# Recutting the last weight load and moving three output products ahead of it in a DMA-bound decode kernel

## The chip, the cores and the metric

The kernel runs on one core of a Trainium2 chip. The metric is the device time of one execution in microseconds (us), the median of several; lower is better. Executions of one kernel scatter by up to about half a microsecond, so differences under that are read from the traces rather than from the times.

The engines are named as in the profile: PE does matmuls, PEld is its weight loads, DVE and ACT are the vector and scalar engines, SP issues the loads. A "row" below means one row of a weight matrix per partition, 128 x 576 numbers in bf16. It takes two matmuls, one for each half of the 576 columns.

## The reference, cut to what matters

```python
x = A_x                                              # (1, 1, 576)
g = _sigmoid((x * gate_w).sum(-1, keepdims=True))
a = _A_ref(x, A_k_cache, A_v_cache, A_wq, A_wo)      # windowed attention, last step: o @ wo
b = _B_ref(x, B_w1, B_b1, B_w2, B_b2)                # gelu(x @ w1 + b1) @ w2 + b2
return g * a + (1 - g) * b                           # (1, 1, 576)
```

One token is decoded. Nearly everything is weights and cache that are read once: 53.6 MB. The last two matrices read are `wo` (4096 x 576) and the second half of `w2` (2304 x 576, so 18 rows on each of 128 partitions).

## The kernel before

The output is a bias and a sum of 68 rows into one accumulator, `y_ps`; each row is a vector column times a weight row. The two halves go to different column tiles of PE.

```python
    def y_add(vec, row, start=False, stop=False):
        for s in range(2):
            last = nc.tensor.matmul(
                y_out[s], lhsT=vec, rhs=row[:, s * DH : (s + 1) * DH],
                start=start, stop=stop, skip_group_check=True,
            )
        return last
```

The end of the stream of loads, all from one queue and in this order:

```python
    for r0, r1 in ((0, 16), (16, RO)):                       # RO = 32
        nc.sync.dma_start(out=wo_t[:, r0:r1, :], in_=wo_src[:, r0:r1, :])
    for j0, j1 in ((0, 10), (10, 16), (16, 18)):             # NJ = 18
        nc.sync.dma_start(out=w2_t[:, NJ + j0 : NJ + j1, :], in_=w2_src[:, 1, j0:j1, :])
```

And the order in which PE takes the rows. Eight rows of `wo` (8 to 15) land with the first half of it but are held back, so that PE has something to do while it waits:

```python
    late = [(gt, f, w2_t[:, f, :]) for f in range(6, NJ)]
    wo_at = [(ov, r, wo_t[:, r, :]) for r in range(RO)]
    w2_at = [(gt, f, w2_t[:, f, :]) for f in range(NJ, NF)]
    late += wo_at[0:8] + wo_at[16:RO] + wo_at[8:13] + w2_at[0:10] + wo_at[13:16] + w2_at[10:]
    before = ov_mm
    for n, (vec, at, row) in enumerate(late):
        with tc.issue_after(before.ins):
            before = y_add(vec[:, at : at + 1], row, stop=(n == len(late) - 1))
    ...
    nc.scalar.copy(out=out_row[:, DH:D], in_=y_out[1])
    nc.vector.tensor_copy(out=out_row[:, 0:DH], in_=y_out[0])
    nc.sync.dma_start(out=out.rearrange("a b d -> (a b) d"), in_=out_row[:])
```

Of the kernel before, what the change touches and what calls it, by code (L numbers as in the profile page):

```python
# [18 lines left out]
def kernel(  # L19
# [564 lines left out]
    RO = Hq * Dh // P  # L584
    wo_t = big.tile([P, RO, D], BF16, name="wo_t", tag="D")
    wo_src = A_wo.rearrange("(p r) n -> p r n", r=RO)
    for r0, r1 in ((0, 16), (16, RO)):
        nc.sync.dma_start(out=wo_t[:, r0:r1, :], in_=wo_src[:, r0:r1, :])  # L588
    for j0, j1 in ((0, 10), (10, 16), (16, 18)):
        nc.sync.dma_start(out=w2_t[:, NJ + j0 : NJ + j1, :], in_=w2_src[:, 1, j0:j1, :])  # L590

    om = const.tile([P, Hq, 4], BF16, name="om")
# [13 lines left out]
    late = [(gt, f, w2_t[:, f, :]) for f in range(6, NJ)]  # L606
    wo_at = [(ov, r, wo_t[:, r, :]) for r in range(RO)]
    w2_at = [(gt, f, w2_t[:, f, :]) for f in range(NJ, NF)]
    late += wo_at[0:8] + wo_at[16:RO] + wo_at[8:13] + w2_at[0:10] + wo_at[13:16] + w2_at[10:]
    before = ov_mm  # L610
    for n, (vec, at, row) in enumerate(late):
        with tc.issue_after(before.ins):
# [36 lines left out]
```

## Time and profile before

| what | before |
|---|---|
| time, median (range) | 132.39 us (132.32 to 132.78), 3 runs |
| span of the profiled run | 130.7 us |
| share of 16 DMA engines used by the load queue | 96.4% |
| PE busy | 79.9 us, 61% |
| chain's last load ends | 127.84 us |
| matmuls behind it | 16, 1.19 us |

How to read it: a queue that holds 96% of the DMA engines means that the kernel is as long as its transfers plus what cannot run beside them. At the end, that is whatever PE must still do with the rows that land last. So the views that matter are the chain of waits, read from its end, and the timeline of PE over the last ten microseconds. The prediction below shows the lines of both.

Beside the views I use the trace's list of landings: each load adds one to a semaphore for each of 16 DMA engines, and the trace holds the time of each increment.

### The profile page before, as it was taken

To read this page: it belongs to the slowest core of one execution; us is meant where nothing else is said; L and a number is where in the kernel's file an instruction comes from. 1 tells how busy PE (TensorE), PEld (TensorE's weight loads), DVE (VectorE), ACT (ScalarE), POOL (GpSimd) and SP (SyncE) were. 2 spreads that over 40 slices of the span, in tenths; PEclk is the share of its full clock that TensorE was granted. 3 is DMA by queue.
4 is the path that set the end of the run, shared out by engine and by line. 5 is a ranking of instruction groups with operands and counts; after the bars stand their busy time and mean duration, and the time that the engine had idled before them with its cause. 6 is when DMAs were issued, how large, how long until landed. Compare 5 with 4: busy or idle time off the path is not lost.

```text
span 130.7 us, 2382 instructions
## 1 busy us (share of the span) xinstructions
PE 79.9 (61%) x1138; PEld 46.0 (35%) x1071; DVE 51.9 (40%) x47; ACT 8.1 (6%) x17; POOL 8.2 (6%) x28
## 2 busy tenths in 40 slices
PE   0037999466002998859909986987100930999573
PEld 0037949366000121211201121677000920945441
DVE  0053000400069969999999995604000010010001
ACT  3000000002100000030003003020000000000001
POOL 6029600000000000000000000000000000000000
PEclk9999999999999999999995999965555555556999
DMA  7999999899899999999999999999989999999980
GB/s 220 431 442 423 474 422 474 372 451 466 381 426 471 401 411 471 411 411 471 421 411 451 441 401 441 413 417 458 456 381 441 461 386 407 434 422 422 398 330 24
DMA packets 2468, 53.75 MB, mean 411 GB/s; under 512 B 278, under 2 KB 282, under 8 KB 540
## 3 DMA queue, kind: packets, MB, share of 16 engines
q1 hardware_dynamic: 2450, 53.61, 96.4%
q8 instruction: 8, 0.13, 0.4%
q10 hardware_dynamic: 10, 0.01, 0.0%
HBM read 53.62 MB, written 0.00 MB: 410 GB/s over the span
## 4 chain that ended last, share of the span: by engine, by line
DMA 54%; DVE 24%; PE 13%; issue 6%; SPq 1%; DVEq 0%
DMA k_t<-in_A_k_cache_dram 27%; DMA w_t<-in_B_w_dram 26%; DVE kt L441 19%; PE s_ps L463 7%; PE o_ps L543 5%; DVE m L479 3%; DVE pt L512 2%; PE y_ps L306 1%; SPq L588 1%; DVE mr L482 1%; PE mt_ps L488 0%; DVE out_row L617 0%; SPq L172 0%; SPq L590 0%; SPq L168 0%
## 5 line engine op out<-in xcount | busy, mean ns | idle before, releaser
L463 PE MATMUL s_ps<-kt,qz_flat 128*128 128x512 bf16 x128 | 32.3, 409 | 17.3 <-DVE kt L441 10.4
L441 DVE STREAM_TRANSPOSE kt<-k_t 128x4096 f32<-128x4096 f32 x8 | 35.3, 4432 | 11.8 <-DMA k_t<-in_A_k_cache_dram 10.7
L543 PE MATMUL o_ps<-pt,v_t 128*128 128x8 bf16 x512 | 14.2, 167 | 16.7 <-DMA v_t<-in_A_v_cache_dram 15.4
L463 PEld LDWEIGHTS <-qz_flat 128*128 128x128 bf16 x64 | 6.8, 106 | 40.1 <-issue 40.0
L543 PEld LDWEIGHTS <-v_t 128*128 128x128 bf16 x512 | 14.1, 103 | 17.5 <-DMA v_t<-in_A_v_cache_dram 15.6
L334 PE MATMUL h_ps<-x,w_t 128*128 128x2 bf16 x162 | 10.4, 202 | 0.0
L334 PEld LDWEIGHTS <-w_t 128*128 128x128 bf16 x162 | 10.2, 162 | 0.5 <-issue 0.4
L306 PE MATMUL y_ps<-w_t,gt 128*1 128x288 bf16 x72 | 7.4, 361 | 1.1 <-DMA w_t<-in_B_w_dram 1.1
L500 ACT ACTIVATE p_t<-s_ps,negm 128x1024 bf16<-128x1024 f32 x4 | 4.5, 1114 | 50.6 <-DVE negm L496 50.6
L573 DVE RECIPROCAL rg<-mt_ps 128x32 f32<-128x32 f32 x1 | 0.4, 358 | 15.8 <-PE mt_ps L568 15.8
L512 DVE STREAM_TRANSPOSE pt<-p_t 128x1024 bf16<-128x1024 bf16 x4 | 4.9, 1224 | 2.7 <-ACT p_t L500 2.7
L372 PE MATMUL q_ps<-x,wq_t 128*128 128x2 bf16 x144 | 4.0, 166 | 3.1 <-DMA wq_t<-in_A_wq_dram 3.1
L306 PE MATMUL y_ps<-wo_t,ov 128*1 128x288 bf16 x64 | 4.9, 299 | 1.4 <-DMA wo_t<-in_A_wo_dram 1.4
L343 DVE COPY hacc<-h_ps 128x36 f32<-128x36 f32 x1 | 0.2, 196 | 13.2 <-PE h_ps L334 13.2
L617 DVE CAST out_row<-y_ps 1x288 bf16<-1x288 f32 x1 | 0.4, 445 | 12.3 <-PE y_ps L306 12.3
L479 DVE TENSOR_REDUCE m<-s_ps 128x1 f32<-128x1024 f32 x4 | 4.8, 1196 | 1.1 <-PE s_ps L463 1.1
L255 PE MATMUL xs_ps<-one_b,rows 1*128 1x1 bf16 x9 | 0.7, 196 | 7.2 <-DVE rows L249 7.2
L372 PEld LDWEIGHTS <-wq_t 128*128 128x128 bf16 x144 | 3.9, 104 | 3.2 <-DMA wq_t<-in_A_wq_dram 3.2
L306 PEld LDWEIGHTS <-gt 128*1 128x1 bf16 x72 | 3.6, 97 | 3.8 <-issue 1.9
L306 PEld LDWEIGHTS <-ov 128*1 128x1 bf16 x64 | 3.1, 90 | 2.9 <-issue 1.7
L593 DVE TENSOR_TENSOR om<-o_ps,rgh 128x128 bf16<-128x128 f32 x1 | 0.3, 291 | 8.6 <-PE o_ps L543 8.6
L249 DVE COPY rows<-rows 1x1152 bf16<-1x1152 bf16 x1 | 0.7, 748 | 6.4 <-DMA rows<-in_A_x_dram 6.4
(64 smaller groups left out, 33.5 us busy)
## 6 DMA issues: line engine op xcount, KB each, us to landing
k_t<-in_A_k_cache_dram SPq DMA_DIRECT2D x4, 4096.0 KB, 33.8
v_t<-in_A_v_cache_dram SPq DMA_DIRECT2D x4, 4096.0 KB, 23.3
wq_t<-in_A_wq_dram SPq DMA_DIRECT2D x1, 4608.0 KB, 26.1
wo_t<-in_A_wo_dram SPq DMA_DIRECT2D x2, 2304.0 KB, 30.0
w_t<-in_B_w_dram SPq DMA_DIRECT2D x1, 2880.0 KB
w_t<-in_B_w_dram SPq DMA_DIRECT2D x1, 2592.0 KB
w_t<-in_B_w_dram SPq DMA_DIRECT2D x1, 2304.0 KB, 8.0
w_t<-in_B_w_dram SPq DMA_DIRECT2D x1, 1440.0 KB
```

What stands on the lines that cost most here:

```text
L249: nc.vector.tensor_copy(out=xdup.rearrange("p (d t) -> p d t", t=2), in_=x_row.rearrange("p (d o) -> p d o", o=1).to_broadcast([1, D, 2]),)
L306: last = nc.tensor.matmul(y_out[s], lhsT=vec, rhs=row[:, s * DH : (s + 1) * DH], start=start, stop=stop, skip_group_check=True,)
L334: nc.tensor.matmul(h_ps[:, j:NF:NJ], lhsT=w1_t[:, i, j:FH:NJ], rhs=x2[:, i, :], start=False, stop=(i == NI - 1 and j == NJ - 1), skip_grou ...
L372: nc.tensor.matmul(q_ps[:, j : Hq : Hq // 2], lhsT=wq_t[:, i, j * Dh : (j + 1) * Dh], rhs=x2[:, i, :], start=(i == 0 and j == 0), stop=(i ...
L441: lambda: nc.vector.transpose(out=kt[g, f][:].bitcast(FP32), in_=keys.rearrange("p c d -> p (c d)").bitcast(FP32),),
L463: last = nc.tensor.matmul(s_ps[g][:, u * 512 : (u + 1) * 512].rearrange("p (c k) -> p c k", k=32), lhsT=qz(g, j, 2 * f + half), rhs=kv[:, ...
L479: queue("dve", lambda: nc.vector.reduce_max(out=m1[:], in_=s_ps[g][:], axis=AX.X))
L482: lambda: nc.vector.tensor_scalar(out=mr[:], in0=hi16[:], scalar1=m1[:, 0:1], scalar2=None, op0=ALU.mult),
L500: nc.scalar.activation(out=p_t[:].rearrange("p c k -> p (c k)"), in_=s_ps[g][:], func=ACT.Exp, bias=negm[:, 0:1], scale=SCALE, accum_out=s ...
L512: lambda: nc.vector.transpose(out=pt[:, g, :, :].rearrange("p c q -> p (c q)"), in_=p_t[:].rearrange("p c k -> p (c k)"),),
L543: last = nc.tensor.matmul(o_ps[:, 8 * g : 8 * g + 8, 0], lhsT=v_t[g][:, c, :], rhs=pt[:, g, c % 32, 8 * (c // 32) : 8 * (c // 32) + 8], st ...
L588: nc.sync.dma_start(out=wo_t[:, r0:r1, :], in_=wo_src[:, r0:r1, :])
```

## The change

The intent: the first of the three pieces gets 12 rows instead of 10, so that less is left for the pieces behind it, and all eight held rows run ahead of the first piece, so that PE is free when the pieces land.

```diff
-    for j0, j1 in ((0, 10), (10, 16), (16, 18)):
+    for j0, j1 in ((0, 12), (12, 16), (16, 18)):
         nc.sync.dma_start(out=w2_t[:, NJ + j0 : NJ + j1, :], in_=w2_src[:, 1, j0:j1, :])
@@
-    late += wo_at[0:8] + wo_at[16:RO] + wo_at[8:13] + w2_at[0:10] + wo_at[13:16] + w2_at[10:]
+    late += wo_at[0:8] + wo_at[16:RO] + wo_at[8:16] + w2_at
```

## The prediction

> **What bounds the kernel now.** I read the page first, from the share of each engine down to the chain that ended last, then the timeline of the end, where the change lies.
>
> ```profile
> span 130.7 us, 2382 instructions
> PE 79.9 (61%) x1138; PEld 46.0 (35%) x1071; DVE 51.9 (40%) x47; ACT 8.1 (6%) x17; POOL 8.2 (6%) x28
> ...
> DMA  7999999899899999999999999999989999999980
> GB/s 220 431 442 423 474 422 474 372 451 466 381 426 471 401 411 471 411 411 471 421 411 451 441 401 441 413 417 458 456 381 441 461 386 407 434 422 422 398 330 24
> ...
> q1 hardware_dynamic: 2450, 53.61, 96.4%
> ```
>
> The row of DMA digits is 8 or 9 nearly from end to end, and one queue holds 96.4% of all that the 16 DMA engines could do. The kernel is a stream of 53.6 MB. What is not hidden behind it is the start and what follows the last landing. No engine comes near: the busiest, PE, has 61%.
>
> The chain of waits says the same of the end. Its columns are start, duration, and what it was:
>
> ```profile
> 93.23 34.61 DMA w_t<-in_B_w_dram
> 127.84 0.04 issue
> 127.89 1.19 PE y_ps L306 x16
> 129.07 0.43 DVE out_row L617
> ```
>
> From 93.23 to 127.84 us the chain is only the load of the last matrix (the second half of w2, 18 rows per partition). After it come 16 matmuls, the copy of the result and the store. The timeline of PE shows the same stretch:
>
> ```profile
> 122.29 2.74 PE L306 MATMUL y_ps<-wo_t,ov 128*1 128x288 bf16 x42 [1.35 <-DMA wo_t<-in_A_wo_dram]
> 125.77 1.39 PE L306 MATMUL y_ps<-w_t,gt 128*1 128x288 bf16 x20 [0.74 <-DMA w_t<-in_B_w_dram]
> 126.99 0.54 PE L306 MATMUL y_ps<-wo_t,ov 128*1 128x288 bf16 x6
> 127.89 1.15 PE L306 MATMUL y_ps<-w_t,gt 128*1 128x288 bf16 x16 [0.36 <-DMA w_t<-in_B_w_dram]
> ```
>
> A row is two matmuls. So: 21 output rows (the second half of wo and five of the eight held back), a wait of 0.74 us, the 10 rows of the first w2 piece, the last three held rows, a wait of 0.36 us, and the last 8 rows, 6 of the second piece and 2 of the third.
>
> This view hides one thing. The last 16 matmuls look like one block behind the second piece, because no idle time lies between them. The trace's list of landings (one semaphore increment for each of 16 DMA engines) has the last increments at 125.727 us for the first piece, 127.844 for the second and 128.578 for the third. The first matmul that waits for each starts at 125.769, 127.885 and 128.619, each 0.041 to 0.042 us later. At the pace of 0.122 us a row (a row starts at 128.372, the next at 128.494) the third piece's first row would have started at 128.616 anyway. So the second and the third piece are both binding, to within 0.003 us. That decides this case.
>
> **What the Trainium skill says.** (1) "DMA: Bandwidth & Descriptors", section "Why a DMA increments its semaphore by 16 and not by 1": the engines finish separately, and only the sixteenth increment means that the data is there. The trace agrees: the first piece's increments run from 123.794 to 125.727 us, and PE moves 0.042 us after the last. (2) The same page, "Queues, rings and completion order": each DMA engine takes its descriptors in ring order. Then cutting the same rows elsewhere does not alter what each engine moves before its very last byte. The trace fits: the pieces land in the order of issue, all issued before 95 us. (3) "TensorE: Matmul & The Clock Gate", "Part 3: Packing small matmuls", "The mechanism": matmuls in different tiles of the array run beside each other, their starts about 4 ns apart. The two halves of a row go to different column tiles, and the trace shows them starting at 125.890 and 125.894 us. So a row, not a matmul, is the unit of cost. (4) The same page, "What's actually happening": the clock drops to half after an idle window of about 3.4 us and comes back after a busy one. Here the granted clock was 0.50 for 34.13 us, up to 120.07 us, and 1.00 after it. That matters for one rival.
>
> **The change part by part.**
>
> *Piece sizes.* 10, 6 and 2 rows become 12, 4 and 2. Bytes, number of loads, issue order and number of packets (128 a piece) stay. The packet records give medians of 435, 266 and 95 ns for 11,520, 6,912 and 2,304 bytes. From the first two, 169 ns for 4,608 bytes, or 85 ns for the two rows that move from one packet to another. The first piece's packet grows to about 520 ns, the second's falls to about 181; the sum is unchanged. The first piece lands later: its two extra rows take 2 x (127.844 - 125.727) / 6 = 0.706 us, so 126.433. By the packets it is 8 packets on each engine x 85 = 0.68 us, nearly the same. The second piece ends at the same row 16 as before: 127.844. The third: 128.578.
>
> *Order.* The comparison of the two programs' instructions has as many on each engine; on PE only the places of six output matmuls change, with their weight loads. The three held rows, formerly between the first and second pieces, now run ahead of the first. So, with R = 0.122 us a row:
>
> Before, starts of what follows the last row: first piece 125.769 + (10 + 3 + 8) R = 128.33; second 127.885 + 8 R = 128.86; third 128.619 + 2 R = 128.86. The latest decides: 128.86.
>
> After: the held rows are ready and have time: 24 rows from 122.29 end issuing at 122.29 + 24 R = 125.22, well ahead of 126.433. Then: first piece 126.433 + 0.042 + (12 + 4 + 2) R = 128.67; second 127.885 + 6 R = 128.62; third 128.619 + 2 R = 128.86. The latest decides: again 128.86.
>
> In order of time: PE waits for the first piece from about 125.40 (last result) to 126.475, does 12 rows until 127.94, finds the second piece there (127.885, so its wait goes), does 4 rows until 128.43, and is held for the third until 128.619. The wait of 0.36 us is not won. Idle before the first piece grows from 0.74 to about 1.07 us, and 0.19 us of pace is held up at the third piece (only some 0.03 us of it appears as idle, since a matmul's span of about 0.285 us covers the rest). The sum is 0.00 us. PE has gained 0.19 us of room in front of a landing that it cannot move.
>
> **The rivals.**
>
> *The gain is real (-0.05 to -0.19 us).* In the old kernel PE has no slack at the third piece: where the second lands late relative to the third, PE's 6 rows (0.73 us) end the program. The new kernel needs only 4 rows there. The interval between those landings is 0.734 us in this one execution; if in others it is shorter, the change wins the difference, up to 0.19 us or 0.14%. For it: the exact tie. Against it: the last packets come at the DMA engines' pace, 8 packets x 95 = 0.76 us on each, which has little reason to shrink. It would give about 132.3.
>
> *PE becomes the bound (+0.1 to +2 us).* The path behind the first landing now has only 0.19 us of room. If the first piece lands 0.2 us later than worked out, each further tenth counts. Much worse would be half clock: rows then cost 0.244 us, and the end would be 126.475 + 18 x 0.244 = 130.87, against 125.769 + 21 x 0.244 = 130.89 of the old order; both lose 2 us alike. Only if the longer single wait dropped the clock at the next step, 126.90 us (120.07 + 2 x 3.413), would the new kernel lose alone: about 3.5 rows done, 14.5 x 0.244 = 3.54 us to go, 130.44, so 1.6 us or 1.2%. Against it: the stretch 120.07 to 123.49 has PE busy for 2.07 of 3.42 us and was followed by full clock; the stretch up to 126.90 would still have about 2.34 of 3.41.
>
> ```profile
> 120.07:123.49 3.42, 2.07 (x33) 1.32 (x31) 0.00 (x0) 0.00 (x0) 0.00 (x0) 1.00 1.00 414
> 123.49:126.90 3.41, 2.67 (x46) 1.79 (x42) 0.00 (x0) 0.00 (x0) 0.00 (x0) 1.00 0.91 372
> ```
>
> (Columns: stretch, length, busy of PE, PEld, DVE, ACT and POOL, granted clock, DMA share, GB/s.)
>
> *The transfers themselves change (-0.2 to +0.2 us).* Other packet sizes might run differently beside each other at the end. The durations are nearly proportional to the bytes and the number of packets is equal, so I give it little.
>
> **Range and chances.** I predict the old median, less a trifle for the first rival: 132.37 us. The three times before lie between 132.32 and 132.78, so the scatter of single runs (0.46 us) is larger than any effect worked out here; a range of 132.1 to 132.75 covers the gain of 0.19, a loss of about that much, and the scatter. A change of 2% is 2.65 us. The DMA stream forbids that gain, as all waits in the stretch together are 0.74 + 0.36 = 1.10 us; the worst rival costs 1.6 to 2. So 0.985 for within 2%, 0.005 faster, 0.01 slower.
>
> **What would show it right or wrong.** In the new profile: one block of 48 output matmuls from about 122.3 us; idle of about 1.07 us before the first w2 block, which starts near 126.47; no wait of note for the second piece; the last four matmuls start at the third landing plus 0.04 us, which stays near 128.6; and the chain's last DMA now ends at the third landing, near 128.6 instead of 127.84, with about 0.45 us of matmuls behind it. Wrong if the last landing itself moves by more than 0.2 us, if the granted clock falls below 1.00 behind 122 us, or if the first piece lands behind 126.65, so that PE runs without a stop from it to the end.

## The result, and the profile after

The changed kernel took 132.44 us (132.37 to 132.56, 4 runs), the kernel before in the same rounds 132.41 us (132.32 to 132.78, 4 runs). The ratio is 0.9998, 95% interval 0.9977 to 1.0019: the same. (A ratio is the mean time of one kernel's fast runs over the mean of the other's fast runs of the same rounds, so it is not quite the ratio of the medians quoted.)

The page of the changed kernel, its span, granted PE clock, DMA and load queue:

```profile
span 130.6 us, 2382 instructions
...
PEclk9999999999999999986999999995555555557999
DMA  6999999899799899999989989899989989999980
...
q1 hardware_dynamic: 2450, 53.61, 96.3%
```

The trace has no record of the clock before 43.98 us, so the digits ahead of it are not a reading: matmuls of one form, 128x512, start 0.427 us apart just before that time and 0.217 us apart just after it, as if the clock had been half until then.

The stream is as full as it was: 96.3% of the DMA engines, the same number of packets and bytes. The end of the chain of waits (start, duration, what):

```profile
92.76 33.55 DMA w_t<-in_B_w_dram
126.31 0.04 issue
126.36 2.12 PE y_ps L306 x32
128.48 0.02 issue
128.50 0.45 PE y_ps L306 x4
```

And the timeline of PE (start, duration, operation, count, and in brackets the idle time before it and what ended it):

```profile
122.19 3.10 PE L306 MATMUL y_ps<-wo_t,ov 128*1 128x288 bf16 x48 [1.73 <-DMA wo_t<-in_A_wo_dram]
126.36 2.56 PE L306 MATMUL y_ps<-w_t,gt 128*1 128x288 bf16 x36 [1.06 <-DMA w_t<-in_B_w_dram]
```

Where there were two waits, 0.74 and 0.36 us, there is one of 1.06 us; where there were four blocks of matmuls, there are two. The order did what it was written for: all 24 output rows run as one block, and PE then works through all 18 rows of the last matrix without a visible stop. And the end is where it was.

The views hide why. The chain steps from the first piece's landing (126.31 us) straight to the end, as if PE's 36 matmuls were the bound. But there is a step of 0.02 us called "issue" at 128.48, just ahead of the last four matmuls. The list of landings explains it. In us from the start of the span:

| kernel | 1st piece landed | 2nd | 3rd | third piece's first row starts | after its landing | copy of the result starts |
|---|---|---|---|---|---|---|
| before | 125.727 | 127.844 | 128.578 | 128.619 | 0.041 | 129.063 |
| after | 126.312 | 127.726 | 128.458 | 128.501 | 0.043 | 128.943 |

In both kernels the last two rows start as soon as the last piece has landed, and not before. In the new one the row ahead of them starts at 128.189, so at the pace of 0.122 us PE was ready at 128.311 and was held up for 0.19 us. The view shows only 0.02 us of that as idle, because a matmul's span in it (about 0.285 us) reaches far beyond the time after which the next could start. The landings of the "after" trace are all about 0.1 us early, those of the second half of `wo` too (122.148 against 122.249), which no part of the change touches: scatter between executions.

The granted clock of the last stretches (columns: stretch, length, busy of PE, PEld, DVE, ACT, POOL, granted clock, DMA share, GB/s) stayed full through the longer wait:

```profile
122.49:125.90 3.41, 2.81 (x46) 1.89 (x43) 0.00 (x0) 0.00 (x0) 0.00 (x0) 1.00 0.98 405
125.90:129.31 3.41, 2.53 (x36) 1.52 (x35) 0.37 (x1) 0.33 (x1) 0.00 (x0) 1.00 0.35 138
```

### The profile page after: what moved, and what is told of

It reads as the page before. It is cut to its first block, busy times and chain, and to the rows that moved or that the text cites. A ratio compares the mean times of both kernels' runs of the same rounds, so it can differ in the third digit from the quotient of the medians.

```text
span 130.6 us, 2382 instructions
## 1 busy us (share of the span) xinstructions
PE 78.9 (60%) x1138; PEld 45.3 (35%) x1071; DVE 51.9 (40%) x47; ACT 8.1 (6%) x17; POOL 8.2 (6%) x28
## 3 DMA queue, kind: packets, MB, share of 16 engines
q1 hardware_dynamic: 2450, 53.61, 96.3%
## 4 chain that ended last, share of the span: by engine, by line
DMA 61%; DVE 21%; PE 10%; issue 6%; SPq 1%; DVEq 0%
DMA k_t<-in_A_k_cache_dram 31%; DMA w_t<-in_B_w_dram 26%; DVE kt L441 15%; PE o_ps L543 5%; DMA rows<-in_A_x_dram 4%; PE s_ps L463 3%; DVE m L479 3%; PE y_ps L306 2%; DVE pt L512 2%; SPq L588 1%; DVE mr L482 1%; DVE out_row L617 0%; PE mt_ps L488 0%; DVE negm L496 0%; DVEq L441 0%
## 5 line engine op out<-in xcount | busy, mean ns | idle before, releaser
L306 PE MATMUL y_ps<-wo_t,ov 128*1 128x288 bf16 x64 | 4.4, 286 | 1.7 <-DMA wo_t<-in_A_wo_dram 1.7
```

Source lines behind the costliest of these rows:

```text
L306: last = nc.tensor.matmul(y_out[s], lhsT=vec, rhs=row[:, s * DH : (s + 1) * DH], start=start, stop=stop, skip_group_check=True,)
```

## The experiments

The theory: the end is the last landing, plus 0.041 us, plus the rows that stand behind that landing (two, 0.122 us each), plus copy and store. PE's own work is hidden up to 0.19 us ahead of that. The rivals: PE's work from the first landing is the bound; or the sizes of the pieces change the transfers; or nothing on PE matters at all. The runs below were made on three occasions, each with its own runs of the kernel before (132.32, 132.57 and 132.38 us median). All results were correct against the reference. The smaller effects are read from the intervals and, above all, from the traces, each of which is one execution.

### One part of the change at a time

**The order alone**, with the old pieces:

```diff
-    for j0, j1 in ((0, 12), (12, 16), (16, 18)):
+    for j0, j1 in ((0, 10), (10, 16), (16, 18)):
```

> The new order with the old pieces of 10, 6 and 2 rows (R = 0.122 us a row). My theory, that the last landing (L3) plus 0.041 us plus two rows sets the end: the second piece is 6 rows and L2 + 0.041 + 8 R ties with L3 + 0.041 + 2 R, so 132.4 us, ratio 1.000. PE waits for about 0.33 us before the first piece (from about 125.4 to 125.7), runs its 10 rows, then waits for about 0.75 us for the second piece, and the last two rows start within 0.02 us of L3 + 0.041. Rival, that the order alone is worth something (the held rows filled a hole usefully): 0.1 to 0.4 us slower.

Measured: 132.40 us (5 runs), ratio 1.0004 (0.9991 to 1.0018). The timeline of PE in this run:

```profile
122.15 3.10 PE L306 MATMUL y_ps<-wo_t,ov 128*1 128x288 bf16 x48 [1.74 <-DMA wo_t<-in_A_wo_dram]
125.63 1.39 PE L306 MATMUL y_ps<-w_t,gt 128*1 128x288 bf16 x20 [0.37 <-DMA w_t<-in_B_w_dram]
127.74 1.14 PE L306 MATMUL y_ps<-w_t,gt 128*1 128x288 bf16 x16 [0.72 <-DMA w_t<-in_B_w_dram]
```

The two waits trade lengths, 0.74 and 0.36 for 0.37 and 0.72, and their sum stays. The last two rows start at 128.472, 0.042 us behind the third landing (128.430). The order by itself is worth nothing, and costs nothing.

**The sizes alone**, with three held rows still behind the first piece:

```diff
-    late += wo_at[0:8] + wo_at[16:RO] + wo_at[8:16] + w2_at
+    late += wo_at[0:8] + wo_at[16:RO] + wo_at[8:13] + w2_at[0:12] + wo_at[13:16] + w2_at[12:]
```

> The new pieces of 12, 4 and 2 rows with three held output rows still between the first and the second piece. My theory: first landing + 0.042 + (12 + 3 + 6) R = about 0.18 us behind L3 + 0.041 + 2 R, so PE runs without a stop from the first piece to the end, the first row of the third piece starts about 0.2 us (0.15 to 0.25) after its landing instead of 0.04, and the time is 0.18 us over the kernel before (ratio 1.001, under what five rounds resolve; the trace decides). Rival, that any order does since the stream is the bound: third piece's first row again at L3 + 0.04 us.

Measured: 132.55 us (5 runs), ratio 1.0020 (1.0007 to 1.0032), so 0.26 us over the kernel before. Its timeline of PE:

```profile
126.65 1.63 PE L306 MATMUL y_ps<-w_t,gt 128*1 128x288 bf16 x24 [1.44 <-DMA w_t<-in_B_w_dram]
128.12 0.54 PE L306 MATMUL y_ps<-wo_t,ov 128*1 128x288 bf16 x6
128.48 0.90 PE L306 MATMUL y_ps<-w_t,gt 128*1 128x288 bf16 x12
```

From the first landing on PE never waits again. The third piece landed at 128.735 us and its first row started at 128.973, 0.238 us later instead of 0.041: a loss of 0.20 us, where 0.18 was worked out. With these sizes and the old order PE is the bound. So the bigger first piece needs the new order, which then merely takes the loss away again.

### How much room PE has, and where

**Eight idle rows ahead of the first piece**: output products with a zero vector, which leave the sum as it is.

```diff
+    zv = const.tile([P, 1], BF16, name="zv")
+    nc.gpsimd.memset(zv[:], 0.0)
-    late += wo_at[0:8] + wo_at[16:RO] + wo_at[8:16] + w2_at
+    late += wo_at[0:8] + wo_at[16:RO] + wo_at[8:16]
+    late += [(zv, 0, wo_t[:, n, :]) for n in range(8)] + w2_at
```

> The new kernel with eight more rows of output products, against a zero vector, ahead of the first piece: 8 R = 0.98 us more PE work. My theory: it lies in the wait of 1.06 us before the first landing, so the time stays (ratio 1.000, 132.4 us), and the wait shrinks to about 0.1 us. Rival, that PE work near the end costs what it takes: 0.98 us more, ratio 1.0074.

Measured: 132.41 us (5 runs), ratio 1.0008 (0.9996 to 1.0021); 1.0074 is ruled out. The timeline of PE, in which 0.05 us of the wait is left where about 0.1 was expected:

```profile
125.22 1.15 PE L306 MATMUL y_ps<-wo_t,zv 128*1 128x288 bf16 x16
126.42 2.53 PE L306 MATMUL y_ps<-w_t,gt 128*1 128x288 bf16 x36
```

A whole microsecond of added work vanished in the wait ahead of the first piece, and the third piece's first row still started 0.042 us behind its landing (128.547 and 128.505).

**The same eight rows ahead of the last two:**

```diff
-    late += wo_at[0:8] + wo_at[16:RO] + wo_at[8:16] + w2_at
+    late += wo_at[0:8] + wo_at[16:RO] + wo_at[8:16] + w2_at[0:16]
+    late += [(zv, 0, w2_t[:, NJ + n, :]) for n in range(8)] + w2_at[16:]
```

> The new kernel with the same eight extra rows placed just ahead of the last two rows. My theory: PE has 0.19 us of room before the third landing, so 0.98 - 0.19 = 0.79 us more (ratio 1.006), and the third piece's first row starts 0.83 us after its landing. Rival, that PE is hidden behind the stream throughout: ratio 1.000. Rival, that PE has no room there, being the bound from the first landing: 0.98 us, ratio 1.0074.

Measured: 133.17 us (5 runs), ratio 1.0070 (1.0057 to 1.0084). The times do not tell 0.79 us (1.0060) from 0.98 us (1.0074); the trace does. Its timeline of PE:

```profile
126.39 2.12 PE L306 MATMUL y_ps<-w_t,gt 128*1 128x288 bf16 x32 [1.07 <-DMA w_t<-in_B_w_dram]
128.34 1.15 PE L306 MATMUL y_ps<-w_t,zv 128*1 128x288 bf16 x16
129.32 0.41 PE L306 MATMUL y_ps<-w_t,gt 128*1 128x288 bf16 x4
```

The third piece landed at 128.483 and its first row started at 129.323, 0.840 us later. Less the usual 0.042 that is 0.80 us of loss for 0.98 us of work: the room is 0.18 us, as worked out. The same work is free at one place and costs four fifths of its length at another, in a kernel in which the DMA engines are 96% busy.

### What stands behind the last landing

**Two pieces, 12 and 6 rows:**

```diff
-    for j0, j1 in ((0, 12), (12, 16), (16, 18)):
+    for j0, j1 in ((0, 12), (12, 18)):
```

> The new order with the last matrix in two pieces, 12 and 6 rows, so that six rows instead of two stand behind the last landing. My theory: the last landing stays where it was (about 128.5 us in the trace) and the end is four rows later: 4 x 0.122 = 0.49 us, ratio 1.0037. Rival, that packet sizes of the last pieces matter, larger packets being quicker: the last landing moves forward by 0.1 us or more and takes back part of it. Rival, that the cut is of no account: ratio 1.000.

Measured: 132.86 us (5 runs) against 132.57 us, ratio 1.0027 (1.0012 to 1.0042), so 0.36 us, with the predicted 0.49 inside the interval. The timeline of PE:

```profile
126.26 1.64 PE L306 MATMUL y_ps<-w_t,gt 128*1 128x288 bf16 x24 [1.05 <-DMA w_t<-in_B_w_dram]
128.35 0.90 PE L306 MATMUL y_ps<-w_t,gt 128*1 128x288 bf16 x12 [0.46 <-DMA w_t<-in_B_w_dram]
```

The last landing was at 128.312 us, 0.15 us earlier than in the changed kernel. Of this 0.10 us is already there at the first piece (126.215 against 126.312), which leaves 0.05 us that the larger packets may have won, less than two executions scatter. From the last landing to the copy it is 0.976 us instead of 0.485: 0.49 us more, exactly four rows.

**One piece of 18 rows:**

```diff
-    for j0, j1 in ((0, 12), (12, 16), (16, 18)):
+    for j0, j1 in ((0, 18),):
```

> The new order with the last matrix in one piece of 18 rows. My theory: the last landing stays at about 128.5 us and all 18 rows stand behind it: 16 x 0.122 = 1.95 us more, ratio 1.0147, if the clock stays full. The wait of PE is then some 3.1 us long (125.4 to 128.5); if the granted clock falls to half in it, as after the idle stretches before 120 us, the rows take 0.244 us each and the loss is up to 4.1 us, ratio 1.031.

Measured: the profiled execution 134.20 us, the five timed ones 135.66 to 136.01; ratio 1.0225 (1.0189 to 1.0260). Two kinds of execution, so two more looks at the same kernel:

> The kernel with the last matrix in one piece again, for a second trace: its first profiled execution took 134.2 us with full clock to the end, the timed ones 135.7 to 136.0. My theory: in the others the granted clock falls to half in or after the wait of 3.1 us, so rows behind the landing cost 0.244 us for part of the block. If this execution is a long one, the block of 36 matmuls takes 3.5 us or more instead of 2.37 and the clock in it is below 1.00. Rival: the landing is later in the long ones, with the clock at 1.00.

> The same once more, for a third trace. Expected as for the second: a time of about 135.8 us goes with a granted clock below 1.00 behind 128 us and a block of 36 matmuls of 3.5 us or more; a time of about 134.2 us goes with full clock and 2.4 us.

Measured: 135.52 and 135.90 us, both of the long kind (single looks, state unknown). The block of matmuls in the timeline of PE, in the short execution:

```profile
128.38 2.37 PE L306 MATMUL y_ps<-w_t,gt 128*1 128x288 bf16 x36 [3.08 <-DMA w_t<-in_B_w_dram]
```

and in the second, with the busy times by stretch (columns as above):

```profile
128.27 3.78 PE L306 MATMUL y_ps<-w_t,gt 128*1 128x288 bf16 x36 [3.06 <-DMA w_t<-in_B_w_dram]
```

```profile
124.36:127.77 3.41, 0.84 (x14) 0.47 (x11) 0.00 (x0) 0.00 (x0) 0.00 (x0) 1.00 0.69 292
127.77:131.18 3.41, 2.91 (x26) 1.62 (x27) 0.00 (x0) 0.00 (x0) 0.00 (x0) 0.50 0.00 0
```

The landing is the same (128.335, 128.223 and 128.338 us in the three traces) and so is the wait, 3.1 us. The clock is not: in the second and the third it was 0.50 for one step of 3.41 us, from 127.77 and from 128.42 us on, and the 36 matmuls took 3.78 us in the second and 4.04 in the third instead of 2.37. Both causes are thus accounted for: sixteen more rows behind the landing (1.95 us worked out; the short execution's copy began 1.96 us later relative to its landing than the changed kernel's, 2.445 against 0.485), and half clock in the two long looks (1.4 to 1.7 us more). The five timed executions were not traced; their times are those of the long kind.

Why an execution is long or short can be read too. The granted clock changes in steps of 3.41 us, and where the steps lie differs between executions. In the short one they cut the wait in two, and PE was busy for half of each step or more:

```profile
123.57:126.98 3.41, 1.73 (x30) 1.13 (x25) 0.00 (x0) 0.00 (x0) 0.00 (x0) 1.00 0.88 377
126.98:130.40 3.42, 2.02 (x34) 1.47 (x35) 0.00 (x0) 0.00 (x0) 0.00 (x0) 1.00 0.04 18
```

In the long ones a step lay mostly or almost wholly within the wait: from 124.36 us with 0.84 us busy, and in the third look from 125.00 us with 0.34.

**The last row alone**, pieces of 12, 4, 1 and 1, the version that the theory would choose:

```diff
-    for j0, j1 in ((0, 12), (12, 16), (16, 18)):
+    for j0, j1 in ((0, 12), (12, 16), (16, 17), (17, 18)):
```

> The new kernel with pieces of 12, 4, 1 and 1 rows, so that one row instead of two stands behind the last landing. My theory: L + 0.041 + 1 R, 0.12 us sooner, less what smaller packets cost: two of 1,152 bytes at 51 ns against one of 2,304 at 95, 7 ns x 8 packets = 0.06 us. So 0.06 us faster, ratio 0.9995, not to be told from 1.000 by the times; in the trace the last row starts 0.04 us after its landing and the copy of the result begins about 0.37 us after the landing instead of 0.49. Rival, that one more load costs more at the end than it gives: last landing 0.2 us later or more.

Measured: 132.30 us (5 runs) against 132.38 us, ratio 0.9992 (0.9979 to 1.0004): the same. In the trace the last landing was at 128.496, the last row started at 128.539 and the copy at 128.859: 0.363 us from the landing to the copy instead of 0.485, the one row expected. It is the best median of all kernels here, but the interval includes 1 and I do not call it faster.

One more thing shows over these runs: each further piece lengthens the transfer a little. From the landing of the second half of `wo` to the last landing it is 6.17 to 6.18 us with one piece (three traces), 6.25 with two (one trace), 6.26 to 6.33 with three (six traces) and 6.37 with four (one trace). The packets fit: the medians of the packets that carry the 18 rows of a partition sum to 774, 786, 794.5 and 802.5 ns, and with 8 on each engine a further piece costs by them an estimated 0.06 to 0.1 us. So it pays only where it takes more than that from behind the last landing; the last row alone, with 0.12 us, just does.

### What holds the last landing where it is

In both traces the 16 increments of each of the last pieces come in two groups of eight. The gap between the groups is 1.0 us before and 1.3 us after; on the average the late eight are 1.4 to 1.5 us behind the early eight. In the changed kernel the third piece's are at 126.59 to 126.95 and 128.23 to 128.46 us. Half of the DMA engines are done 1.5 us before the end. Following this back through the loads of the changed kernel's trace, together with the queue that fetches PE's instructions (8 packets of 16 KB, about 1.05 us each):

| load landed at (us) | instruction fetches begun by then | engines early / late |
|---|---|---|
| 14.73 | 0 | 16 / 0 |
| 26.97 | 1 | 15 / 1 |
| 36.68 | 2 | 14 / 2 |
| 46.57 to 85.46 | 3 | 13 / 3 |
| 91.69 | 4 | 12 / 4 |
| 101.41 | 5 | 11 / 5 |
| 111.13 | 6 | 10 / 6 |
| 116.64 | 7, the last begun at 115.32 | 10 / 6 |
| 122.15 | 8, the last begun at 121.55 | 9 / 7 |
| 126.31 and on | 8 | 8 / 8 |

The early engines are done with a load about 1.5 us before it lands, and the last fetch of the rows 116.64 and 122.15 began after that, so it does not show in that load yet. So I suspected that each fetch holds up one DMA engine. Two runs bear on this.

**The third piece on 8 engines.** Its source is written as 8 groups of 16 partitions. "DMA: Bandwidth & Descriptors", section "Why a DMA increments its semaphore by 16 and not by 1", states that the number of engines is the largest up to 16 that divides the slowest dimension of both sides, and that on this path they are the lowest-numbered ones. The number is tested here; which engines they are, no run here shows.

```diff
+    def last_piece_on_half(nc):
+        ...                     # find the last weight load in the built program
+        halves = [[step * n // 8, 8], [step, n // 8], [one, size]]
+        whole = [list(dst.ap[0]), [1, 1], list(dst.ap[1])]
+        kept[at] = copy.replace(
+            load, ins=[copy.replace(src, ap=halves)], outs=[copy.replace(dst, ap=whole)],
+            ant_dge_precooked=False,
+        )
+    nc.at_finalize(last_piece_on_half)
```

> The new kernel with the third piece (two rows) carried by 8 of the 16 DMA engines instead of all (its source written as 8 groups of 16 partitions[...]). In both traces 8 engines post their increments about 1.3 us after the other 8, and there were 8 instruction fetches of 16 KB by then, the number of late engines growing by one with each fetch. If the chosen eight are the ones without a fetch: they finish 8 more packets of 95 ns, 0.76 us, after 127.0, so at about 127.75, the others end with the second piece at 127.73, and the end comes 0.7 us sooner: ratio 0.995. If they are the ones with a fetch: the last landing moves out by 0.73 us, ratio 1.0055. If some of each: again about 0.73 us later, with the 8 increments in two groups. If the number of engines isn't changed by this: nothing, 16 increments as before.

Measured: 133.90 us (4 runs), ratio 1.0101 (1.0084 to 1.0119), 1.3 us slower. The timeline of PE:

```profile
128.70 0.65 PE L332 MATMUL y_ps<-w_t,gt 128*1 128x288 bf16 x8 [0.53 <-DMA w_t<-in_B_w_dram]
129.99 0.41 PE L332 MATMUL y_ps<-w_t,gt 128*1 128x288 bf16 x4 [0.64 <-DMA w_t<-in_B_w_dram]
```

There were 8 increments, as the page's rule for the number has it, and they came in two groups: six from 128.12 to 128.84 us and two at 129.90 and 129.95. By these groups the chosen eight are a mixture, six early and two late, and the late ones set the end. The loss is larger than the 0.73 us worked out, for two reasons that the trace shows: the second piece landed late, 2.16 us behind the first instead of 1.41, and the third piece's packets took 139 ns each (median) instead of 94.5. Why, the run does not tell: the edit also sets `ant_dge_precooked=False`, with which this load took 0.72 us to issue instead of 0.43, and that change and the crowding on half of the engines came together in it.

**A ninth fetch**: 128 tiny products with their weight loads, 256 instructions, placed where PE waits for a load anyway.

```diff
     queue("pe", lambda: value_products(1))
+    queue("pe", idle_products)     # 128 matmuls of 128x2 by alternating zero columns
```

> The new kernel with 256 more PE instructions (128 tiny matmuls by a zero vector and their weight loads) in the stretch of 93 to 99 us where PE waits for a load anyway. My theory of the late DMA engines, that each fetch of PE instructions (16 KB) holds up one DMA engine for about 1.3 us and each fetch takes another engine: nine fetches instead of eight, and the increments of the last pieces come in groups of 7 and 9 instead of 8 and 8, 1.3 us apart; the last landing and the time stay (132.4 us, ratio 1.000, if the extra matmuls fit the stretch). Rival, that the late engines have another cause (their place, or the loads themselves): 8 and 8 as before. Should the ninth fetch fall on an engine that had one: one increment 2.6 us behind, and 1.3 us more time.

Measured: 135.25 us median (134.03 to 135.40, 4 runs), ratio 1.0186 (1.0146 to 1.0225). The page's line for instruction fetches shows nine packets, and the timeline of PE a much later second half of `wo`:

```profile
q8 instruction: 9, 0.15, 0.4%
```

```profile
123.88 5.85 PE L308 MATMUL y_ps<-wo_t,ov 128*1 128x288 bf16 x48 [3.29 <-DMA wo_t<-in_A_wo_dram]
129.57 2.37 PE L308 MATMUL y_ps<-w_t,gt 128*1 128x288 bf16 x36
```

My first expectation, groups of 7 and 9 and no loss, was wrong; the case that I had put last came true, with 1.3 us forecast for it. The ninth fetch fell on an engine that had had one. The third piece's increments are 8 from 126.57 to 127.22, 7 from 128.08 to 128.45, and one at 129.99 us. The last landing moved by 1.53 us (129.986 against 128.458) for 256 instructions that do nothing, on an engine with time to spare. The rival, that the late engines have another cause, would have left 8 and 8. The early fill is a check on this: its trace has nine fetches as well, but the ninth began at 130.03 us, behind the last landing, and its groups are 8 and 8.

The other 1.50 us came from the clock. Waiting longer for `wo`, PE was at 0.50 from 122.70 to 129.53 us, the 48 matmuls took 5.85 us instead of 3.10, and the last row pair started 1.54 us behind the landing. Together 3.03 us, which is what this execution lost (135.40 against 132.38 us). The quickest of the four, 134.03 us, is near what the landing alone would give (132.38 + 1.53 = 133.91); it was not traced. The stretch ahead of the fall (columns as above), with 1.29 us of PE's work in it, where the changed kernel, whose `wo` had landed by then, has 1.69 and stayed at full clock:

```profile
119.29:122.70 3.41, 1.29 (x21) 0.70 (x16) 0.00 (x0) 0.00 (x0) 0.00 (x0) 1.00 0.98 413
```

## Why the prediction was right

**The time.** 132.37 us was predicted with 132.1 to 132.75; 132.44 was measured, and the ratio of 0.9998 is a change of 0.00 within its interval. The time by itself proves little, since any effect under the scatter would have met this range; what follows is what bears the mechanism out.

**Piece sizes.** The first landing was put 0.706 us later; relative to the landing of `wo`, which the change does not touch, it moved from 3.478 to 4.164 us, 0.686 later. The packets were expected at 520 and 181 ns and took 520 and 180 (medians). Second and third kept their places: between their landings lie 0.734 us before and 0.732 after.

**Order.** The block of 48 matmuls began at 122.19 us; the wait before the first piece was expected to be 1.07 us and is 1.06. The second piece's wait went. PE was expected to be 0.05 us behind the second landing and its row started at 127.821, 0.054 us later than it could have. The room before the third landing was 0.19 us, expected and measured, and the late fill confirms it with 0.18.

**The tie.** Everything rested on reading the old kernel's last 16 matmuls as two groups, with the third piece binding as well as the second. Two things show that this is so. The change takes two rows, 0.24 us, from the path behind the second landing and gains nothing. And in the order-only run the row ahead of the third piece's starts at 128.347 us, so that PE at its pace was ready at 128.469, within 0.003 us of the 128.472 at which the row behind the third landing started.

**The rivals.** That other executions would have a shorter interval between second and third landing, and so a gain, is not borne out: it is 0.732 to 0.736 us in the six traces before, after, order only, sizes only, early and late fill. PE as the bound is what the sizes alone bring, 0.20 us. The fall of the clock did not occur in the changed kernel's trace, but does where the wait is three times as long (the single piece, 3.1 us). That piece sizes alter the transfers is not seen with three pieces: from the landing of `wo` to the last it is 6.33 us before and 6.31 after. Their number does seem to, by the estimate of 0.06 to 0.1 us a piece above.

**One step was wrong.** The prediction says that "the chain's last DMA now ends at the third landing, near 128.6". It ends at the first landing, 126.31 us, since the chain follows visible idle time and PE's wait for the third piece shows only as 0.02 us. The mechanism was right, but the view named for checking it could not show it; the landings could.

What stays open: why the third piece on half of the engines ran at 139 ns a packet, and whether the last load could be laid on the engines that had no fetch. In that run six of the eight were early ones, but which, this trace does not say.

## What to carry to other kernels

At the end of this stream of loads, the time was the last landing plus the work that stood behind it, as long as PE had room ahead of that landing, and only that work was worth cutting: rows behind the last landing cost their full 0.122 us each, rows ahead of an earlier wait cost nothing. Look for ties before trusting a visible wait: two landings can bind within a few nanoseconds of each other, and then removing one wait only uncovers the other, which the idle time in the timeline may not show at all. And in a DMA-bound kernel ask what else uses the DMA engines; here the fetches of PE's own instructions put half of the engines about 1.5 us behind the other half.

## What the Trainium skill lacked or had wrong

- "Runtime: NRT & Kernel Launch", "Instruction fetch mechanics", calls the cost of crossing a 16 KiB boundary of instructions mostly hidden. For the engine that runs them it may be; for a kernel bound by DMA it was not: each fetch put one DMA engine about 1.5 us behind, 8 of 16 by the end, and a ninth fetch moved the last landing by 1.53 us. No page says that instruction fetches delay the loads that share an engine with them.
- "TensorE: Matmul & The Clock Gate", "What's actually happening", has the clock fall after an idle window of about 3.4 us and gives no share of busy time at which a window counts as idle. Here it fell after windows that were only mostly idle: with PE busy for 0.84 of 3.41 us (single piece, second look), for 1.29 (ninth fetch) and for 1.44 (early fill, 74.77 to 78.18 us). It stayed full after 1.46 (kernel before, 55.22 to 58.63 us) and 1.69 (changed kernel). The profile's busy time is not all that counts, though: in the kernel before, the clock fell at 85.94 us after a window that is listed as busy for 3.41 of 3.41 us, with 116 matmuls that are nearly all of 8 columns.
- "DMA: Bandwidth & Descriptors", "Why a DMA increments its semaphore by 16 and not by 1": the rule for the number of engines held (8 increments), but no page tells that packets on half of the engines, with `ant_dge_precooked` off, may take 139 ns instead of 94.5 for 2,304 bytes.
